# Windowed attention with a gated feed-forward layer: the probabilities of units 3 to 15 turned by VectorE and a DRAM round trip instead of TensorE

## Chip, cores and metric

One core of one Trainium2 chip runs the whole program. The metric is the device time of one execution in microseconds (us). The kernel before took 1105.88 us (median of three runs, 1104.23 to 1106.31).

## Reference

Inputs q, k, v are float32 of shape (8, 8, 576, 64): batch, head, position, head dimension. Heads 0 to 3 look back over a plain window of 32 positions, heads 4 to 7 over 32 positions four apart. The attention output, laid out as 4608 tokens of 512 features, goes through an RMS norm and a gated feed-forward layer of width 1536.

```python
scores = scale * np.matmul(q, k.transpose(0, 1, 3, 2))
mask_plain = (rel >= 0) & (rel < window)
mask_dil = (rel >= 0) & (rel < window * dilation) & (rel % dilation == 0)
scores = np.where(masks[None, :, :, :], scores, -1000000000.0)
attn = np.exp(scores - max); attn = attn / (sum + 1e-09)
x = np.matmul(attn, v)            # then tokens x 512
xn = x / rms * rms_g
out = (silu(xn @ w_gate) * (xn @ w_val)) @ w_out
```

## The kernel before, in words

The 4608 tokens are cut into 16 units of 288 (half a batch element each). Unit u's attention runs while unit u-1's feed-forward layer is on TensorE, so attention is the side work and the feed-forward matmuls fill TensorE.

**Feed-forward.** A unit takes 36 steps: for each of 12 column blocks j a gate step, a val step and a proj step (`gate`, `val`, `proj`). From unit 1 on, each step is 12 matmuls of 288 columns (L679, L682): numbers are split into a high and a low float32r part and three products are summed. VectorE works in it at L724 (silu), L737 (product), and in the norm; ScalarE at L719 (tanh) and L748 (high part); GpSimd at L749 (low part).

**Attention bursts.** A unit has 14 bursts; a burst (u, c, i) is a block of 96 or 72 queries of two heads. Bursts with c = 0, 1 are plain (96 queries, 128 or 96 keys), those with c = 2, 3 are dilated (72 queries; 104 keys in odd units, 72 in even ones). The small matmuls of a burst stand at the end of a step. With q the step of its scores:

- step q: scores (`scored`, L524), into the one PSUM buffer `s`;
- q+1: `scores_max` on VectorE: L381 adds the mask to the low product, L386 (once for each head, with a read of the accumulator behind it) adds the high product and keeps the row's extreme. The result is tile `t` (96 x 2 x 128);
- q+2: exponential on ScalarE (L401);
- q+4: sum and reciprocal on VectorE (L410, L411), scaling by it on GpSimd (L417);
- q+6: two TensorE transposes against an identity (`transposed`, L497) into a part of PSUM; from there ScalarE copies the high part (L477) and VectorE subtracts for the low part (L479) into `pt`, in which keys are the partitions;
- q+10: probabilities times values (`output`, L512); at q+11 VectorE adds up the four partial results into `xraw` (`take`, L439 and L441, once for each head).

From unit 3 on the scores of a unit's bursts are two steps apart, from 11 steps before the feed-forward of the unit ahead of it begins to step 15 of that (`EARLY`, `LAST`); `BEHIND` sets the two later places. The first three units take other schedules and plain float32 products.

**Order.** The order of every engine is written by hand: `later(dt, rank, fn)` puts work into the flush at the beginning of step now+dt, sorted by rank; the engines run their queues in order. All DMAs are issued from SP: a query/key tile for each head (L293), a value tile for each burst (`load_v`, L301), the outputs (L777). `split` makes high and low parts of queries and keys, `split_v` those of the values.

Of the kernel before, what the change touches and what calls it, by code (L numbers as in the profile page):

```python
# [57 lines left out]
EARLY, LAST = -11, 15  # L58
BEHIND = 6, 10
DONE = 25  # L60
# [17 lines left out]
def attn_moe(ctx: ExitStack, tc: tile.TileContext, qk_in, v_in, w_gate, w_val, w_out, rms_g, outT):  # L78
# [7 lines left out]
    sb = ctx.enter_context(tc.tile_pool(name="sb", bufs=2))  # L86
    ps = ctx.enter_context(tc.tile_pool(name="ps", bufs=1, space=PSUM))


# [224 lines left out]
    def split_v(b, dt):  # L314
        k = everything.index(b) % 2

        def hi():
            if k not in vparts:
                vparts[k] = late[0].tile([P, 2, 2, D], F32R, name=f"vhl_{k}", bufs=1)
            A.copy(out=vparts[k][:, :, 0], in_=vs[b])  # L320

        def lo():
            vp = vparts[k]
            G.tensor_tensor(out=vp[:, :, 1], in0=vs.pop(b), in1=vp[:, :, 0], op=ALU.subtract)  # L324
            load_v(further(b, 3))

        later(dt, 3.3, hi)
        later(dt, 5.1, lo)
# [6 lines left out]
    def split(u, h, when, ek, eq):  # L335


        raw = heads[u, h]
        _, _, nkt = geometry(u, h // 2)
        qr, kr = raw[:, :U], raw[:, U:U + nkt]  # L340
        got = []

        def tile(cols, tag):
            pool, bufs = (late[0], 1) if late and h % 4 == 3 else (sb, 3)
            return pool.tile([P, cols], F32R, tag=tag, name=f"{tag}_{u}_{h}", bufs=bufs)

        def k_hi():
            ks = tile(2 * KW, "ks").rearrange("p (t k) -> p t k", t=2)
            A.copy(out=ks[:, 0, :nkt], in_=kr)
            got.append(ks)  # L350

        def k_lo():
            ks = got[0]
            ek.tensor_tensor(out=ks[:, 1, :nkt], in0=kr, in1=ks[:, 0, :nkt], op=ALU.subtract)  # L354

        def q_hi():
            qs = tile(U, "qs")
            A.copy(out=qs, in_=qr)  # L358
            got.append(qs)

        def q_lo():
            ks, qs = got
            eq.tensor_tensor(out=qs[D:], in0=qr[D:], in1=qs[D:], op=ALU.subtract)  # L363
            heads[u, h] = (qs, ks)
            if after(u, h, 2):
                load(*after(u, h, 2))
# [7 lines left out]
    def scores_max(u, c, i, s_ps):  # L374
# [3 lines left out]
        other = u < NNAT and everything.index((u, c, i)) % 4 == 3  # L378
        t = sb.tile([QB, 2, P], F32, tag="qs" if other else "t", name=f"t_{u}_{c}_{i}", bufs=3)
        if u >= NEX:  # L380
            V.tensor_tensor(out=t[:nq, :, :n], in0=sv[:nq, :, 1, :n],  # L381
                            in1=mask[:nq, None, mc:mc + n].to_broadcast([nq, 2, n]), op=ALU.add)
        sm = sums[everything.index((u, c, i)) % len(sums)]
        for a in range(2):
            plus = t[:nq, a, :n] if u >= NEX else mask[:nq, mc:mc + n]
            V.tensor_tensor_reduce(out=t[:nq, a, :n], in0=sv[:nq, a, 0, :n], in1=plus,  # L386
                                   op0=ALU.add, op1=ALU.min,
                                   scale=-(0.5 if u == NNAT else 1.0) / math.sqrt(D),
                                   scalar=3e38, accum_out=sm[:nq, a, 0:1])
        st[u, c, i] = t, sm  # L390

    def by_rows(u, c, i):
# [3 lines left out]
    def scores_exp(u, c, i):  # L396
# [3 lines left out]
        for a in range(2):  # L400
            A.activation(out=t[:nq, a, :n], in_=t[:nq, a, :n], func=AF.Exp, scale=-1.0,  # L401
                         bias=sm[:nq, a, 0:1], accum_out=None if by_rows(u, c, i) else sm[:nq, a, 1:2])

    def scores_norm(u, c, i):
# [7 lines left out]
        for a in range(2):  # L412
            if u == 1:
                later(1, -0.5, lambda a=a: A.activation(out=t[:nq, a, :n], in_=t[:nq, a, :n], func=AF.Copy,
                                                        scale=sm[:nq, a, 3:4]))
                continue
            (V if u == 0 and (c, i) > (NC - 1, 1) else G).tensor_scalar(  # L417
                out=t[:nq, a, :n], in0=t[:nq, a, :n], scalar1=sm[:nq, a, 3:4],
                scalar2=1.0, op0=ALU.mult, op1=ALU.mult)
# [50 lines left out]

    def untranspose(b, t_ps, wait):
        blocks, nq, _ = geometry(*b[:2])
        n = blocks[b[2]][3]
        t_in = t_ps[:n].rearrange("k (a q) -> k a q", a=2)[:, :, :nq]
        exact = b[0] < NEX
        st[b] = pt = sb.tile([P, 2, 2, QB], F32 if exact else F32R, tag="pt", name=f"pt_{b[0]}_{b[1]}_{b[2]}", bufs=2)
        A.copy(out=pt[:n, 0, :, :nq], in_=t_in)  # L477
        def low_part():
            V.tensor_tensor(out=pt[:n, 1, :, :nq], in0=t_in, in1=pt[:n, 0, :, :nq], op=ALU.subtract)  # L479

        if not exact:
            later(1, 0.4 if wait > 1 else -1.5, low_part) if wait else low_part()

    def products(q, t, o, t_ps, s_tag="s", o_tag="o", wait=0):
# [41 lines left out]
        order = ((t, transposed), (o, output), (q, scored))  # L526
        if t and t[0] >= NEX:
            order = ((o, output), (t, transposed), (q, scored))
        parts = [(b, fn, a) for b, fn in order for a in range(2)]
# [3 lines left out]
        if t:  # L533
            later(1, 0.2, lambda: untranspose(t, t_ps, wait))
        if o:
# [5 lines left out]
            if o[0] < NEX:  # L541
                later(1, 9, lambda: load_v(further(o, 3)))
            far = further(o, 2)
            if far and far[0] >= NEX:
                split_v(far, 8 if o[0] < NEX else 1)
        if q:
# [3 lines left out]
            later(3 if q[0] < NNAT else 4, 1 if behind else -1, lambda: scores_norm(*q))  # L550
            u, c, i = q
            nxt = after(u, 2 * c, 2)
            nb = len(geometry(u, c)[0])
# [275 lines left out]
    for u in range(1, NU):  # L829
        q_at = [LAST - (LAST - EARLY) * (nb - 1 - k) // (nb - 1) for k in range(nb)]  # L830
        t_at, o_at = ([t + n for t in q_at] for n in BEHIND)
        if u <= NNAT:
# [25 lines left out]
    for u in range(NU):  # L858
        for j in range(NJ):
            for part in range(0 if u + j else 2, 3):  # L860
# [16 lines left out]
                else:  # L877
# [3 lines left out]
                    free = None  # L881
                if part == 2 or part == 1 and events.get(now[0], {}).get("t", (0,))[0] >= NEX:
                    if "t" in events.get(now[0], {}):
                        free = ps.tile([P, 512], F32, tag=bank("g", j), name=f"t_{u}_{j}")[:, :2 * QB]
                attend(free, s_tag="acc2" if t < 4 else "s", wait=(1, 2, 0)[part])
# [71 lines left out]
```

## Time and profile before

| | before |
|---|---|
| median of 3 runs | 1105.88 us |
| profiled execution | 1103.95 us |
| its span, first to last instruction | 1102.2 us |
| TensorE matmul busy | 1095.2 us (99%) |
| VectorE busy | 782.7 us (71%) |
| ScalarE busy | 614.8 us (56%) |
| GpSimd busy | 670.1 us (61%) |
| 16 DMA engines, share of the span | 24.3% |

PE is TensorE's matmul side, DVE is VectorE, ACT ScalarE, POOL GpSimd, SP the engine that issues DMAs. A share over the span is a mean over fuller and emptier stretches; the view of windows gives the busy time in any stretch, and the view of waits gives what an engine waited for there. From some 164 us to the end of the span a unit takes about 66 us, 18 burst places of two steps each, of which 14 carry bursts.

### The profile page before, as it was taken

The numbers are of one execution on the slowest core, as the hardware profiler recorded it, in microseconds if no ns is written. First come the engines' busy times: TensorE is split into PE (matmuls) and PEld (weight loads), VectorE is DVE, ScalarE is ACT, GpSimd is POOL, SyncE is SP. The second block draws the span as 40 slices with busy tenths as digits, with TensorE's granted clock in tenths as the row PEclk, the third lists the DMA queues.
The fourth block names the chain that finished last, engine by engine and source line by source line (L and its number), as shares of the span: only waits on it lengthen the run. The fifth ranks groups of instructions, "written<-read, shape, count | busy, mean of one in ns | idle before, by whom it ended". The sixth has DMA issues, their size and how long they took to land.

```text
span 1102.2 us, 25627 instructions
## 1 busy us (share of the span) xinstructions
PE 1095.2 (99%) x8416; PEld 1071.6 (97%) x8416; DVE 782.7 (71%) x3094; ACT 614.8 (56%) x2202; POOL 670.1 (61%) x1152
## 2 busy tenths in 40 slices
PE   8999999999999999999999999999999999999998
PEld 7787999999999999999999999999999999999998
DVE  7988667868687676867768677686867768687412
ACT  6895676556465564646556464664646556464211
POOL 6333589657585675757657575775758657584211
PEclk9999999999999999999999999999999999999999
DMA  9774213212131131312212131131212212120000
GB/s 255 205 263 163 79 51 87 74 35 82 43 94 52 41 97 30 95 42 73 66 36 85 43 94 43 50 96 37 79 43 83 64 32 83 53 74 13 18 6 22
DMA packets 61543, 82.18 MB, mean 75 GB/s; under 512 B 7298, under 2 KB 41090, under 8 KB 61410
## 3 DMA queue, kind: packets, MB, share of 16 engines
q1 hardware_dynamic: 61410, 80.54, 24.3%
q8 instruction: 67, 1.10, 0.4%
q14 instruction: 66, 0.54, 0.2%
HBM read 71.08 MB, written 9.44 MB: 73 GB/s over the span
## 4 chain that ended last, share of the span: by engine, by line
PE 95%; POOL 2%; DVE 1%; ACT 1%; issue 1%; POOLq 0%; ACTq 0%; DVEq 0%
PE acc L682 17%; PE g L682 17%; PE v L682 17%; PE acc L679 9%; PE g L679 9%; PE v L679 9%; PE o L512 3%; PE s L524 3%; PE acc L676 2%; PE v L676 2%; PE g L676 2%; PE t L497 2%; PE s L521 1%; PE g L497 1%; PE busy L802 1%; PE o L509 1%
## 5 line engine op out<-in xcount | busy, mean ns | idle before, releaser
L749 POOL TENSOR_TENSOR hlo<-th,hhi 128x288 fp32r<-128x288 f32 x179 | 145.2, 811 | 161.3 <-ACT hhi L748 147.8
L401 ACT ACTIVATE t<-t,sum 96x128 f32<-96x128 f32 (+3 forms) x448 | 165.9, 374 | 107.8 <-DVE sum L386 105.1
L682 PE MATMUL acc<-hhi,lo 128*128 128x288 f32 x720 | 212.7, 295 | 0.0
L417 POOL TENSOR_SCALAR t<-t,sum 96x128 f32<-96x128 f32 (+3 forms) x416 | 147.6, 366 | 88.4 <-DVE sum L411 74.6
L719 ACT ACTIVATE th<-g 128x288 f32<-128x288 f32 x180 | 73.8, 410 | 195.2 <-PE g L682 100.5
L682 PE MATMUL g<-xhi,lo 128*128 128x288 f32 x612 | 180.3, 295 | 0.0
L682 PE MATMUL v<-xhi,lo 128*128 128x288 f32 x612 | 180.2, 294 | 0.0
L439 DVE TENSOR_REDUCE xraw<-o 64x72 f32<-64x144 f32 (+1 forms) x364 | 117.1, 322 | 84.0 <-PE o L512 79.5
L724 DVE SCALAR_TENSOR_TENSOR th<-th,g 128x288 f32<-128x288 f32 x180 | 80.8, 449 | 102.0 <-ACT th L719 78.4
L682 PEld LDWEIGHTS acc<-hhi,lo 128*128 128x128 f32 x720 | 135.4, 188 | 0.0
L324 POOL TENSOR_TENSOR vhl<-vt,vhl 128x128 fp32r<-128x128 f32 x182 | 84.4, 464 | 70.4 <-ACT vhl L320 66.8
L748 ACT CAST hhi<-th 128x288 fp32r<-128x288 f32 x180 | 77.7, 432 | 75.5 <-DVE th L737 74.6
L682 PEld LDWEIGHTS g<-xhi,lo 128*128 128x128 f32 x612 | 115.2, 188 | 0.0
L682 PEld LDWEIGHTS v<-xhi,lo 128*128 128x128 f32 x612 | 115.1, 188 | 0.0
L737 DVE TENSOR_TENSOR th<-th,v 128x288 f32<-128x288 f32 x180 | 79.8, 444 | 43.6 <-PE v L682 43.5
L441 DVE TENSOR_TENSOR xraw<-o,xraw 64x72 f32<-64x72 f32 (+1 forms) x364 | 101.1, 278 | 12.5
L679 PE MATMUL acc<-hhi,hi_o 128*128 128x288 f32 x360 | 109.0, 303 | 0.0
L679 PE MATMUL g<-xhi,hi_g 128*128 128x288 f32 x357 | 107.0, 300 | 0.0
L682 PE MATMUL acc<-hlo,hi_o 128*128 128x288 f32 x360 | 106.4, 296 | 0.0
L363 POOL TENSOR_TENSOR qs<-qk,qs 64x288 fp32r<-64x288 f32 x104 | 84.3, 811 | 24.1 <-ACT qs L358 16.9
L354 POOL TENSOR_TENSOR ks<-qk,ks 128x288 fp32r<-128x288 f32 (+2 forms) x104 | 96.8, 936 | 3.1
L682 PE MATMUL g<-xlo,hi_g 128*128 128x288 f32 x322 | 95.1, 295 | 0.0
(193 smaller groups left out, 3458.6 us busy)
## 6 DMA issues: line engine op xcount, KB each, us to landing
qk<-in_qk_dram SPq DMA_DIRECT2D x60, 288.0 KB, 2.9
vt<-in_v_dram SPq DMA_DIRECT2D x196, 64.0 KB, 1.9
qk<-in_qk_dram SPq DMA_DIRECT2D x30, 352.0 KB, 2.9
out_dram<-ot SPq DMA_DIRECT2D x64, 144.0 KB, 1.9
qk<-in_qk_dram SPq DMA_DIRECT2D x30, 304.0 KB, 2.9
raw<-in_w_gate_dram SPq DMA_DIRECT2D x12, 512.0 KB, 4.6
raw<-in_w_val_dram SPq DMA_DIRECT2D x12, 512.0 KB, 3.3
raw<-in_w_out_dram SPq DMA_DIRECT2D x12, 512.0 KB, 4.2
```

Source lines behind the costliest of these rows:

```text
L324: G.tensor_tensor(out=vp[:, :, 1], in0=vs.pop(b), in1=vp[:, :, 0], op=ALU.subtract)
L354: ek.tensor_tensor(out=ks[:, 1, :nkt], in0=kr, in1=ks[:, 0, :nkt], op=ALU.subtract)
L363: eq.tensor_tensor(out=qs[D:], in0=qr[D:], in1=qs[D:], op=ALU.subtract)
L401: A.activation(out=t[:nq, a, :n], in_=t[:nq, a, :n], func=AF.Exp, scale=-1.0, bias=sm[:nq, a, 0:1], accum_out=None if by_rows(u, c, i) els ...
L417: (V if u == 0 and (c, i) > (NC - 1, 1) else G).tensor_scalar(out=t[:nq, a, :n], in0=t[:nq, a, :n], scalar1=sm[:nq, a, 3:4], scalar2=1.0, ...
L439: V.tensor_reduce(out=ours, in_=o[:D, cols:cols + 2 * nq].rearrange("d (t q) -> d q t", t=2), axis=mybir.AxisListType.X, op=ALU.add)
L441: V.tensor_tensor(out=ours, in0=o[D:, cols:cols + nq], in1=ours, op=ALU.add)
L679: PE.matmul(out, wh[:, cc, :], xh, start=start, stop=False)
L682: PE.matmul(out, w[:, cc, :], v, start=False, stop=stop and k == 1)
L724: V.scalar_tensor_tensor(out=t, in0=t, scalar=1.0, in1=g, op0=ALU.add, op1=ALU.mult)
L737: V.tensor_tensor(out=t, in0=t, in1=v_ps[:, :U], op=ALU.mult)
L749: (V if (u, j) == (NU - 1, NJ - 1) else G).tensor_tensor(out=lo, in0=t, in1=hi, op=ALU.subtract)
```

## The change

From unit 3 on (`u >= NEX`) TensorE no longer transposes the probabilities. Instead, in `turn`:

- `scores_max` writes the keys of a row interleaved by four: key 4i+c goes to column 32c+i. L381's and L386's successors write, and the second also reads, tile `t` in steps of 32 elements. Where a burst has fewer than 96 queries or 128 keys, VectorE first sets the whole tile to zero (96 x 256).
- q+5: VectorE transposes `t` in place in squares of 32 by 32 (96 x 256), rank 4, behind `scores_max` of the burst two places later (rank 0.7).
- q+5, rank 9.5: SP sends the tile to DRAM (192 rows of 512 bytes).
- q+6, rank 9.5: SP fetches it into `pt` (128 partitions, 6 pieces of 128 bytes each).
- q+9: ScalarE makes the high part (rank 0.2) and VectorE the low part (rank 0.9), both now out of SBUF. The output stays at q+10.

`t` gets a fourth buffer, the value tile has two buffers instead of three, and the loads of values and of queries and keys are issued a step later, at rank 9.9, behind the fetch.

```diff
-BEHIND = 6, 10
+OUTPUT = 10
+TURN = (5, 4), (5, 9.5), (6, 9.5), (9, 0.2), (9, 0.9)
...
-            vt = sb.tile([P, 2, D], F32, tag="vt", name=f"vt_{u}_{c}_{i}", bufs=3)
+            vt = sb.tile([P, 2, D], F32, tag="vt", name=f"vt_{u}_{c}_{i}", bufs=2)
...
-            load_v(further(b, 3))
+            later(1, 9.9, lambda: load_v(further(b, 2)))
...
         if u >= NEX:
-            V.tensor_tensor(out=t[:nq, :, :n], in0=sv[:nq, :, 1, :n],
-                            in1=mask[:nq, None, mc:mc + n].to_broadcast([nq, 2, n]), op=ALU.add)
+            if nq < QB or n < P:
+                V.memset(t, 0.0)
+            tk = keys(t, n)
+            V.tensor_tensor(out=tk[:nq], in0=sv[:nq, :, 1, :n].rearrange("q a (i c) -> q a i c", c=4),
+                            in1=mask[:nq, mc:mc + n].rearrange("q (i c) -> q i c", c=4)[:, None].to_broadcast(
+                                [nq, 2, n // 4, 4]), op=ALU.add)
...
+    def keys(t, n):
+
+        return t.rearrange("q a (c i) -> q a i c", i=W)[:, :, :n // 4]
...
+    def turn(b):
+        blocks, nq, _ = geometry(*b[:2])
+        n = blocks[b[2]][3]
+        got = []
+
+        def squares():
+            t = st[b][0]
+            V.transpose(out=t, in_=t)
+
+        def put():
+            t, _ = st.pop(b)
+            d = dr.tile([2, QB, P], F32, tag="turn", name=f"turn_{b[0]}_{b[1]}_{b[2]}")
+            nc.sync.dma_start(out=d.rearrange("a q k -> q a k"), in_=t)
+            got.append(d)
+
+        def get():
+            st[b] = pt = sb.tile([P, 2, 2, QB], F32R, tag="pt", name=f"pt_{b[0]}_{b[1]}_{b[2]}", bufs=2)
+            squares = got.pop().rearrange("a (r i) (c j) -> (i c) (a r) j", i=W, j=W)
+            nc.sync.dma_start(out=pt[:, 1].bitcast(F32).rearrange("k a (r j) -> k (a r) j", j=W), in_=squares)
...
+        for (dt, rank), fn in zip(TURN, (squares, put, get, high, low)):
+            later(dt, rank, fn)
```

VectorE, in unit 7's attention, from the last plain bursts to the third dilated one (t is a burst's scores and later its probabilities, with c and i in the name; o the output in PSUM; pt the turned probabilities), before:

```order
L439 TENSOR_REDUCE xraw_0_6861<-o_0_2_6992 64x96
L441 TENSOR_TENSOR xraw_0_6861<-o_0_2_6992,xraw_0_6861 64x96
L724 SCALAR_TENSOR_TENSOR th_1_6999<-th_1_6999,g_1_6978 128x288
L381 TENSOR_TENSOR t_2_1_7008<-s_2_1_6991,mask 72x2x104
L386 ISA t_2_1_7008,sum_86<-s_2_1_6991,t_2_1_7008 72x104
L386 ISA sum_86 72x1
L386 ISA t_2_1_7008,sum_86<-s_2_1_6991,t_2_1_7008 72x104
L386 ISA sum_86 72x1
L479 TENSOR_TENSOR pt_1_1_7001<-g_1_6978,pt_1_1_7001 128x192
L410 TENSOR_REDUCE sum_90<-sum_90 72x2
L411 RECIPROCAL sum_90<-sum_90 72x2
L737 TENSOR_TENSOR th_1_6999<-th_1_6999,v_1_7022 128x288
```

The same place now, beginning at the silu:

```order
L767 SCALAR_TENSOR_TENSOR th_1_7118<-th_1_7118,g_1_7099 128x288
L387 MEMSET t_2_1_7126 96x256
L389 TENSOR_TENSOR t_2_1_7126<-s_2_1_7112,mask 72x2x26x4
L398 ISA t_2_1_7126,sum_88<-s_2_1_7112,t_2_1_7126 72x26x4
L398 ISA sum_88 72x1
L398 ISA t_2_1_7126,sum_88<-s_2_1_7112,t_2_1_7126 72x26x4
L398 ISA sum_88 72x1
L521 TENSOR_TENSOR pt_1_0_7014<-pt_1_0_7014 128x192
L502 STREAM_TRANSPOSE t_1_2_6980<-t_1_2_6980 96x256
L427 TENSOR_REDUCE sum_92<-sum_92 72x2
L428 RECIPROCAL sum_92<-sum_92 72x2
L780 TENSOR_TENSOR th_1_7118<-th_1_7118,v_1_7141 128x288
```

The zeroing (L387) and the squares (L502) have come in, and the low part (L521, before L479) now belongs to the burst whose output is the next on TensorE, one burst later than before.

TensorE, at the end of a proj step of the same unit (s_2_2 are the scores of the burst after), before:

```order
L682 MATMUL acc_3_7064<-hhi_0_6924,lo_1009 128x288
L512 MATMUL o_1_0_7070<-pt_1_0_6922,vhl_2337 128x192 x2
L497 MATMUL t_1_7068<-ident,t_1_2_6869 128x96 x2
L524 MATMUL s_2_2_7069<-ks_4_6741,qs_4_6768 72x2x104
L524 MATMUL s_2_2_7069<-ks_5_6766,qs_5_6805 72x2x104
L679 MATMUL g_2_7093<-xhi_0_6732,hi_o_1008 128x288
```

and now:

```order
L725 MATMUL acc_3_7186<-hhi_0_7039,lo_1011 128x288
L555 MATMUL o_1_0_7191<-pt_1_0_7014,vhl_2335 128x192 x2
L567 MATMUL s_2_2_7190<-ks_4_6853,qs_4_6882 72x2x104
L567 MATMUL s_2_2_7190<-ks_5_6880,qs_5_6917 72x2x104
L722 MATMUL g_2_7215<-xhi_0_6844,hi_o_1010 128x288
```

Only the two transposes have gone; the output and the scores stand where they stood.

SP, loads around the same bursts (turn is the tile in DRAM, vt the values, qk a head's queries and keys), before:

```order
L293 DMA qk_6_6803<-in_qk_dram 128x704
L293 DMA qk_7_6838<-in_qk_dram 128x704
L301 DMA vt_1_2_6875<-in_v_dram 128x128
L301 DMA vt_2_0_6940<-in_v_dram 128x128
L777 DMA out_dram<-ot_0_6959 128x288
```

and now:

```order
L295 DMA qk_6_6954<-in_qk_dram 128x704
L507 DMA turn_1_0_6988<-t_1_0_6849 96x2x128
L295 DMA qk_7_6990<-in_qk_dram 128x704
L513 DMA pt_1_0_7014<-turn_1_0_6988 128x6x32
L303 DMA vt_1_1_7016<-in_v_dram 128x128
L507 DMA turn_1_1_7058<-t_1_1_6911 96x2x128
L820 DMA out_dram<-ot_0_7076 128x288
```

For each burst a DMA to DRAM and one back have come in, the way back behind a wait for the way there, and the loads of later tiles stand between them.

More of the change, by code (lines that the diff above doesn't have):

```diff
@@ L365, in q_lo @@
             if after(u, h, 2):
-                load(*after(u, h, 2))
+                later(1, 9.9, lambda: load(*after(u, h, 2)))
         for dt, rank, fn in zip(when, (3, 5, 3.1, 0.9 if when[3] > when[2] else 3.2), (k_hi, k_lo, q_hi, q_lo)):
@@ L378, in scores_max @@
         other = u < NNAT and everything.index((u, c, i)) % 4 == 3
-        t = sb.tile([QB, 2, P], F32, tag="qs" if other else "t", name=f"t_{u}_{c}_{i}", bufs=3)
+        if late and everything.index((u, c, i)) % 4 == 3:
+            t = late[0].tile([QB, 2, P], F32, tag="t", name=f"t_{u}_{c}_{i}", bufs=1)
+        else:
+            t = sb.tile([QB, 2, P], F32, tag="qs" if other else "t", name=f"t_{u}_{c}_{i}", bufs=3)
         if u >= NEX:
-            V.tensor_tensor(out=t[:nq, :, :n], in0=sv[:nq, :, 1, :n],
-                            in1=mask[:nq, None, mc:mc + n].to_broadcast([nq, 2, n]), op=ALU.add)
+            if nq < QB or n < P:
[4 more added lines that the diff above has]
+                                [nq, 2, n // 4, 4]), op=ALU.add)
         sm = sums[everything.index((u, c, i)) % len(sums)]
         for a in range(2):
-            plus = t[:nq, a, :n] if u >= NEX else mask[:nq, mc:mc + n]
-            V.tensor_tensor_reduce(out=t[:nq, a, :n], in0=sv[:nq, a, 0, :n], in1=plus,
+            out, scores, plus = t[:nq, a, :n], sv[:nq, a, 0, :n], mask[:nq, mc:mc + n]
+            if u >= NEX:
+                out = plus = tk[:nq, a]
+                scores = scores.rearrange("q (i c) -> q i c", c=4)
+            V.tensor_tensor_reduce(out=out, in0=scores, in1=plus,
                                    op0=ALU.add, op1=ALU.min,
@@ L400, in scores_exp @@
         for a in range(2):
-            A.activation(out=t[:nq, a, :n], in_=t[:nq, a, :n], func=AF.Exp, scale=-1.0,
+            e = t[:nq, a, :n] if u < NEX else t[:nq, a].rearrange("q (c i) -> q c i", i=W)[:, :, :n // 4]
+            A.activation(out=e, in_=e, func=AF.Exp, scale=-1.0,
                          bias=sm[:nq, a, 0:1], accum_out=None if by_rows(u, c, i) else sm[:nq, a, 1:2])
@@ L416, in scores_norm @@
                 continue
+            e = t[:nq, a, :n] if u < NEX else t[:nq, a].rearrange("q (c i) -> q c i", i=W)[:, :, :n // 4]
             (V if u == 0 and (c, i) > (NC - 1, 1) else G).tensor_scalar(
-                out=t[:nq, a, :n], in0=t[:nq, a, :n], scalar1=sm[:nq, a, 3:4],
+                out=e, in0=e, scalar1=sm[:nq, a, 3:4],
                 scalar2=1.0, op0=ALU.mult, op1=ALU.mult)
@@ L469, in attn_moe, with untranspose, high, low @@
     everything = [b for u in range(NU) for b in bursts(u)]
-    def untranspose(b, t_ps, wait):
+    def untranspose(b, t_ps):
         blocks, nq, _ = geometry(*b[:2])
         n = blocks[b[2]][3]
[L474 to L482, printed above, removed]
+        st[b] = pt = sb.tile([P, 2, 2, QB], F32, tag="pt", name=f"pt_{b[0]}_{b[1]}_{b[2]}", bufs=2)
+        A.copy(out=pt[:n, 0, :, :nq], in_=t_ps[:n].rearrange("k (a q) -> k a q", a=2)[:, :, :nq])
+    def turn(b):
[14 more added lines that the diff above has]
+            nc.sync.dma_start(out=pt[:, 1].bitcast(F32).rearrange("k a (r j) -> k (a r) j", j=W), in_=squares)
+        def high():
+            pt = st[b]
+            A.copy(out=pt[:n, 0, :, :nq], in_=pt[:n, 1, :, :nq].bitcast(F32))
+        def low():
+            pt = st[b]
+            V.tensor_tensor(out=pt[:n, 1, :, :nq], in0=pt[:n, 1, :, :nq].bitcast(F32), in1=pt[:n, 0, :, :nq],
+                            op=ALU.subtract)
+        for (dt, rank), fn in zip(TURN, (squares, put, get, high, low)):
+            later(dt, rank, fn)
     def products(q, t, o, t_ps, s_tag="s", o_tag="o", wait=0):
@@ L533, in products @@
         if t:
-            later(1, 0.2, lambda: untranspose(t, t_ps, wait))
+            later(1, 0.2, lambda: untranspose(t, t_ps))
         if o:
@@ L881, in attn_moe @@
                     free = None
-                if part == 2 or part == 1 and events.get(now[0], {}).get("t", (0,))[0] >= NEX:
-                    if "t" in events.get(now[0], {}):
-                        free = ps.tile([P, 512], F32, tag=bank("g", j), name=f"t_{u}_{j}")[:, :2 * QB]
+                if part == 2 and "t" in events.get(now[0], {}):
+                    free = ps.tile([P, 512], F32, tag=bank("g", j), name=f"t_{u}_{j}")[:, :2 * QB]
                 attend(free, s_tag="acc2" if t < 4 else "s", wait=(1, 2, 0)[part])
```

12 lines of the change are left out of this document (7 added, 5 removed).

## The prediction

> **What bounds the kernel now.** I read the page first: the busy times and the chain that ended last.
>
> ```profile
> PE 1095.2 (99%) x8416; PEld 1071.6 (97%) x8416; DVE 782.7 (71%) x3094; ACT 614.8 (56%) x2202; POOL 670.1 (61%) x1152
> PE 95%; POOL 2%; DVE 1%; ACT 1%; issue 1%; POOLq 0%; ACTq 0%; DVEq 0%
> ```
>
> TensorE bounds it: 95% of the chain, hardly ever idle. So an instruction taken from TensorE is worth its whole place there, as long as nothing else becomes late. The second question is therefore who has room for the work that takes its place. The view of windows, for unit 7's bursts in three stretches and for the middle stretch of unit 8:
>
> ```profile
> core 0: us, PE busy (x) PEld busy (x) DVE busy (x) ACT busy (x) POOL busy (x), PEclk, DMA share, GB/s
> 427.91:446.35 18.44, 18.44 (x146) 18.44 (x145) 12.06 (x48) 12.14 (x41) 12.03 (x20) 1.00 0.17 48
> 446.35:479.98 33.63, 33.63 (x272) 33.63 (x271) 28.15 (x123) 20.59 (x79) 26.19 (x46) 1.00 0.31 91
> 479.98:493.99 14.01, 14.01 (x113) 14.01 (x111) 9.08 (x35) 4.92 (x17) 6.30 (x12) 1.00 0.08 20
> 512.34:545.67 33.33, 33.33 (x273) 33.33 (x271) 27.19 (x123) 20.00 (x79) 25.06 (x46) 1.00 0.30 90
> ```
>
> VectorE's 71% is uneven. In the middle stretch, nine burst places long, it is busy for 28.15 of 33.63 us; outside it has 6.4 and 4.9 us over. And not all of the missing 5.5 us is free. The view of waits for VectorE, first in the odd unit's middle stretch, then in the even one's:
>
> ```profile
> DVE xraw L439 <- PE o L512: 2.6, 5, 0.9
> DVE th L737 <- PE v L682: 0.8, 3, 0.3
> DVE xlo L660 <- ACT xhi L659: 0.2, 1, 0.2
> ```
>
> ```profile
> DVE xraw L439 <- PE o L512: 3.1, 5, 1.0
> DVE th L737 <- PE v L682: 1.1, 3, 0.5
> DVE xlo L660 <- ACT xhi L659: 0.2, 1, 0.2
> ```
>
> It waits for only 3.6 us in the odd unit and 4.4 us in the even one; the rest are the small steps between instructions that follow each other. That wait is what VectorE can still take on before TensorE waits for it: 0.4 to 0.5 us a burst.
>
> **What is removed.** The transposes of units 3 to 15:
>
> ```profile
> 160.00:1102.00 942.00, 56.00 (x364) 36.23 (x364) 1.00 0.20 58
> 459.27 0.37 PE L512 MATMUL o<-pt,vhl 128*128 128x192 f32 x2
> 459.48 0.33 PE L497 MATMUL t<-ident,t 96*128 96x96 f32 x2
> 459.59 0.41 PE L524 MATMUL s<-ks,qs 128*72 128x208 f32 x2
> 602.38 0.29 PE L497 MATMUL t<-ident,t 72*104 72x72 f32 x2
> 602.48 0.39 PE L524 MATMUL s<-ks,qs 128*72 128x208 f32 x2
> ```
>
> The first row is the window of line 497 alone: 364 of them, two for each of 182 bursts. Their 56 us busy overlap with their neighbours, so what a pair holds up TensorE is read from start to start: 0.11 us for a plain pair, 0.10 us for a dilated one. 6 of 14 bursts are plain: 78 x 0.11 + 104 x 0.10 = 19 us. That is all the change can win. The copies and the low parts stay (SBUF in place of PSUM as their source, which I cost at nothing; ScalarE, at 20.59 of 33.63 us, covers its own). GpSimd's scaling stays too.
>
> **What is added on VectorE.** Its prices come from the groups by form:
>
> ```profile
> L381 DVE TENSOR_TENSOR t<-s,mask 96x256 f32<-96x256 f32 x66 | 27.5, 417 | 1.2
> L381 DVE TENSOR_TENSOR t<-s,mask 72x208 f32<-72x208 f32 x56 | 20.6, 368 | 1.1
> L386 DVE CUSTOM_DVE_ANT_0 t<-s,t 96x128 f32<-96x128 f32 x132 | 32.9, 284 | 2.3
> L386 DVE CUSTOM_DVE_ANT_0 t<-s,t 72x72 f32<-72x72 f32 x96 | 18.3, 226 | 1.6
> L263 DVE MEMSET qk<- 64x576 f32 x3 | 1.6, 538 | 1.1 <-PEq L945 0.9
> L441 DVE TENSOR_TENSOR xraw<-o,xraw 64x72 f32<-64x72 f32 x208 | 60.5, 291 | 7.2
> L441 DVE TENSOR_TENSOR xraw<-o,xraw 64x96 f32<-64x96 f32 x156 | 40.6, 260 | 5.4
> L435 ACT COPY xraw<-o 64x72 f32<-64x72 f32 x32 | 9.2, 287 | 1.8 <-PE o L509 1.5
> L435 ACT COPY xraw<-o 64x96 f32<-64x96 f32 x24 | 5.6, 232 | 0.2
> ```
>
> *Squares.* No transpose by VectorE is in this trace. The nearest row has the same 96 x 256 elements: 0.42 us. Bounds: 0.33 us, if an operation with one source has a shorter start, and 0.8 us if these elements take two passes. I take 0.42, nine times in the middle stretch: 3.8 us.
>
> *Zeroing.* 96 x 256, in every dilated burst. The only row is 64 x 576 in 0.538 us; by the number of elements 0.24 us; bounds 0.12 us (twice the rate) and 0.33 us. Eight in the stretch: 1.9 us.
>
> *Writing in steps of 32 elements.* No row has that step. Two rows of this kernel have a step of 4 elements, in the 72-query bursts: `take`'s L441 needs 0.291 us for 72 elements in steps against 0.260 us for 96 side by side. L386 loses 58 ns for 56 fewer elements, 1.04 ns each; so 72 side by side would have cost L441 0.235 us, and the step costs 56 ns, 0.78 ns an element. ScalarE's L435 shows the same sign, 0.287 against 0.232 us. If 0.78 ns holds for the add (208 elements in odd units) and for the two halves behind it (2 x 104), a dilated burst pays 0.32 us; in even units (144 and 2 x 72) 0.225 us; a plain one 0.4 us. In the middle stretch (one plain, eight dilated): 3.0 us odd, 2.2 us even. Bounds: nothing, and twice this. I take the row's price.
>
> [...]
>
> *Sum on VectorE in a middle stretch.* Odd units: 3.8 + 1.9 + 3.0 = 8.7 us. Free: 3.6 us less the 9 x 0.1 us by which TensorE gets shorter, 2.7 us. Missing: 6.0 us. Even: 7.9 against 3.5 us, missing 4.4 us. Outside the middle stretch the 6.4 and 4.9 us hold what comes in (five bursts' squares and steps, some 4 us, and two squares).
>
> When VectorE is late, who waits? Its queue runs in order, and an output on TensorE now waits for the low part, which stands behind zeroing, the add and the two halves of a later burst in one flush. So TensorE waits at the output, with scores and feed-forward behind it. A little lateness is covered:
>
> ```profile
> 458.39 0.08 DVE L386 DVE_READ_ACCUMULATOR2_ANT sum<- 72x1 f32 x1
> ```
>
> The scores were taken up by 458.47 us and the next ones wrote their buffer at 459.59, 1.1 us later; with the burst's own zeroing and steps (0.5 us) in between I leave 0.5 us of it once in a unit. So 5.5 us in each of 7 odd units and 3.9 us in each of 6 even ones: 62 us.
>
> **What is added on the queues.**
>
> ```profile
> qk<-in_qk_dram SPq DMA_DIRECT2D x60, 288.0 KB, 2.9
> vt<-in_v_dram SPq DMA_DIRECT2D x196, 64.0 KB, 1.9
> out_dram<-ot SPq DMA_DIRECT2D x64, 144.0 KB, 1.9
> DMA  0000000000000000000000335667541000000000
> DMA packets 144, 0.07 MB, mean 33 GB/s; under 512 B 16, under 2 KB 144, under 8 KB 144
> ```
>
> The way there is like an output: 1.9 us. The way back is 768 pieces of 128 bytes. The last two rows are a window of 2 us around one value tile (128 pieces of 512 bytes): about ten slices of 0.05 us, 0.5 us. Between 1.9 us (a value tile's landing, if the number of pieces costs nothing) and 4.4 us (640 more pieces at that pace, 2.5 us) I take 3 us. With 0.3 us for the high part the chain from the squares to the low part is 4.1 to 6.6 us. VectorE gets to that low part two burst places later (2 x 33.63 / 9 = 7.5 us) less one low part and one squares (some 0.8 us): 6.7 us. So I cost the round trip at nothing; if it lasts longer, ScalarE waits in its queue at the high part, with the exponentials and high parts of the feed-forward behind it. On SP the fetch waits for the landing of the way there, and the loads of values and queries stand behind it. A value tile is wanted some two steps (3.7 us) after its load can go, against 1.9 us. The zeroing waits until the way there has read the buffer's last tile; with four buffers that is some two steps earlier.
>
> **The sum.** 1103.95 (the profiled execution) - 19 + 62 = 1147 us. The median before stands 2 us above that execution, less than the doubt in any price.
>
> **Rivals.**
>
> *VectorE has room; TensorE stays the bound.* Squares at 0.33, zeroing at 0.12 us and a step that is free make 9 x 0.33 + 8 x 0.12 = 3.9 us: 0.7 us missing in odd units after the 0.5 us, none in even ones, 5 us in all: 1103.95 - 19 + 5 = 1090 us. It turns at a gain when the missing time falls under 19 us, that is about 0.56 us added a burst. For it: 71% busy, and all three prices from other operations. Against it: L441, and that the squares alone, at 0.42 us, take more than is free in an odd unit's middle stretch.
>
> *The round trip is late.* If the fetch goes at a value tile's pace and, in the 8 of 14 bursts with a query load on the queue beside it, lands another 1.0 us later (2.9 against 1.9 us), then the low part is late by 1.0 us in 104 bursts: 1103.95 - 19 + 104 = 1189 us. It decides from a landing of about 4.4 us after the issue on. For it: the pieces are 128 bytes, where no row here goes under 512 apart from the DMAs' last words; against it: the DMA engines are used to 0.31 at most. [...]
>
> *Both sides meet.* Missing time of 19 us would leave the time as it is.
>
> **Chances.** VectorE the bound: 0.57, of it 0.42 with the step priced as above (1147 us; at twice that price 7 x 3.0 + 6 x 2.2 = 34 us more, 1181; with squares in two passes 13 x 9 x 0.38 = 44 us more, 1191) and 0.15 with a free step (34 us less, 1113). Room on VectorE, 1090: 0.20. Round trip late, 1189 or more: 0.18. Level: 0.05. Range 1090 to 1215 us: it leaves out the faster half of the second case and the far end of the third. Faster by over 0.2% (2 us, what a measurement here can tell): 0.20; within: 0.05; slower: 0.75.
>
> **What would show it.** In the profile after: no transposes of units 3 to 15 on PE; PE with idle time at the outputs, released by VectorE's low part; in the middle stretches VectorE full, with waits near zero, and the stretch longer by 3 to 5 us than before. The squares near 0.42 us, the add of a dilated odd burst near 0.37 + 0.16 = 0.53 us, the zeroing near 0.24 us. ScalarE's high part should seldom wait for the DMA. I am wrong if PE stays full (then the prices were too high), or if the waits at the output come from the high part and the DMA.

## The result, and the profile after

| | before | after |
|---|---|---|
| median (4 runs each) | 1105.09 us | 1188.24 us (1187.89 to 1191.32) |
| ratio to before, 95% interval | | 1.0758, 1.0736 to 1.0780 |
| profiled execution, span | 1103.95, 1102.2 us | 1187.89, 1185.7 us |
| forecast | | 1147 us, 1090 to 1215 |

The kernel became 83 us slower. The forecast had the direction and the engine; it had 41 us too little. The page of the kernel after, busy times and chain:

```profile
PE 1109.9 (94%) x8052; PEld 1051.8 (89%) x8052; DVE 942.8 (80%) x3392; ACT 627.5 (53%) x2202; POOL 674.1 (57%) x1152
PE 46%; DVE 41%; issue 7%; ACT 3%; DMA 2%; POOL 1%; DVEq 0%; POOLq 0%; ACTq 0%; SPq 0%
```

TensorE has lost its 364 transposes, and with them its place as the only bound: of the chain that ended last, VectorE now has 41%, where it had 1%. The view of windows, for the same three stretches of unit 7 and the middle stretch of unit 8 as in the prediction:

```profile
452.52:470.91 18.39, 18.32 (x143) 18.08 (x141) 14.06 (x49) 11.63 (x41) 12.03 (x20) 1.00 0.24 63
470.91:510.86 39.95, 34.76 (x254) 32.66 (x253) 36.60 (x139) 21.26 (x80) 26.66 (x47) 1.00 0.47 115
510.86:525.71 14.85, 14.11 (x107) 13.75 (x105) 10.88 (x40) 5.55 (x18) 6.50 (x13) 1.00 0.37 84
544.24:582.58 38.34, 34.49 (x255) 32.43 (x254) 34.99 (x139) 21.15 (x80) 25.04 (x47) 1.00 0.48 116
```

The middle stretches are 6.3 and 5.0 us longer, and VectorE is busy in them for 8.45 us more (28.15 to 36.60) and 7.80 us more (27.19 to 34.99). In both, the view of VectorE's waits is empty: it goes from one piece to the next. Who waits instead, in the view of waits over the whole span:

```profile
ACT pt L517 <- DMA pt<-turn: 56.8, 77, 2.7
PE o L555 <- DVE pt L521: 51.3, 83, 1.1
PEld o L555 <- issue: 43.8, 62, 1.3
PEld o L555 <- POOL vhl L326: 15.7, 17, 1.3
PEld g L722 <- DVE th L780: 19.6, 52, 0.5
```

L555 is the output, L521 the low part. In the records of the single instructions, each of 106 late outputs began at most 0.3 us after the end of a low part, most of them 0.26 us after it, 74 us of TensorE in all. So the rows listed under "issue" and under the value parts are for the most part the same wait (the value parts had been ready 3.6 us and more). Another 16 us of idle time stand at the gate steps, which wait for VectorE's product (L780). The prices, in the groups by form of the kernel after:

```profile
L502 DVE STREAM_TRANSPOSE t<-t 96x256 f32<-96x256 f32 x182 | 78.9, 433 | 0.0
L387 DVE MEMSET t<- 96x256 f32 x116 | 31.6, 272 | 7.9
L389 DVE TENSOR_TENSOR t<-s,mask 72x208 f32<-72x208 f32 x56 | 30.4, 543 | 6.2 <-DVE t L387 0.5
L398 DVE CUSTOM_DVE_ANT_1 t<-s,t 72x72 f32<-72x72 f32 x96 | 23.3, 282 | 1.6
```

Squares 0.433 us (forecast 0.42), zeroing 0.272 (0.24), the add of a dilated odd burst 0.543 (0.53). There are 116 zeroings: one for each of the 104 dilated bursts, and 12 for plain bursts with 96 keys, which the prediction left out. Seven of them, not eight, fall into unit 7's middle stretch; the eighth begins at 511.01 us, just behind its end. The round trip, in the view of DMA issues, with the median from issue to landing in the last column:

```profile
turn<-t SPq DMA_DIRECT2D x182, 96.0 KB, 1.8
pt<-turn SPq DMA_DIRECT2D x182, 96.0 KB, 2.2
vt<-in_v_dram SPq DMA_DIRECT2D x196, 64.0 KB, 2.1
```

The way back (96 KB) lands in 2.2 us, about as fast as a value tile (64 KB, 2.1 us).

One price stands in no row above. The low part used to read one of its two sources from PSUM; now it reads both from SBUF. The low part of the norm (`xlo`, L660 before, L703 after) reads both from SBUF in either kernel. Such a piece took longer in these traces when it began while GpSimd was in a subtraction of its own with over 0.16 us to go. The same two pieces of unit 7, GpSimd's (`ks`) and VectorE's (`xlo`), in the view of the timeline, first before:

```profile
447.89 0.46 DVE L660 TENSOR_TENSOR xlo<-xraw,xhi 128x288 fp32r<-128x288 f32 x1 [0.18 <-ACT xhi L659]
447.92 1.37 POOL L354 TENSOR_TENSOR ks<-qk,ks 128x416 fp32r<-128x416 f32 x1
```

and after:

```profile
472.94 1.08 POOL L356 TENSOR_TENSOR ks<-qk,ks 128x416 fp32r<-128x416 f32 x1
473.06 1.28 DVE L703 TENSOR_TENSOR xlo<-xraw,xhi 128x288 fp32r<-128x288 f32 x1
```

Whichever of the two began second was the longer for it: GpSimd's took 1.37 us in place of 1.08, VectorE's 1.28 in place of 0.46. All 7 odd units have the longer `ks` before (1.37 to 1.38 us) and the longer `xlo` after (1.28 to 1.29). Of the 182 low parts of the bursts none took over 0.36 us before, though 144 had a piece of GpSimd beside them and 117 began inside one; now 78 begin inside one, and 30 of these take between 0.40 and 0.91 us, each ended at least 0.16 us after that piece. Of the other 48 one began together with GpSimd's piece, the rest in its last 0.16 us, and none took over 0.37 us. The 182 together take 67.5 us in place of 58.0. No run moved GpSimd's pieces alone, so what this is worth in the end is not measured.

### The profile page after: what moved, and what is told of

Read it like the earlier page. It is cut to its first block, busy times and chain, and to the rows that moved or that the text cites. A ratio compares the mean times of both kernels' runs of the same rounds, so it can differ in the third digit from the quotient of the medians.

```text
span 1185.7 us, 26525 instructions
## 1 busy us (share of the span) xinstructions
PE 1109.9 (94%) x8052; PEld 1051.8 (89%) x8052; DVE 942.8 (80%) x3392; ACT 627.5 (53%) x2202; POOL 674.1 (57%) x1152
## 4 chain that ended last, share of the span: by engine, by line
PE 46%; DVE 41%; issue 7%; ACT 3%; DMA 2%; POOL 1%; DVEq 0%; POOLq 0%; ACTq 0%; SPq 0%
PE g L725 8%; PE v L725 8%; PE acc L725 7%; DVE xraw L457 6%; DVE t L389 6%; DVE xraw L459 5%; PE g L722 4%; PE v L722 4%; PE acc L722 3%; DVE t L398 3%; DVE pt L521 3%; DVE th L780 3%; DVE t L502 3%; DVE th L767 3%; DVE t L387 3%
## 5 line engine op out<-in xcount | busy, mean ns | idle before, releaser
L435 POOL TENSOR_SCALAR t<-t,sum 96x128 f32<-96x128 f32 (+3 forms) x416 | 150.3, 373 | 200.8 <-DVE sum L428 170.9
L457 DVE TENSOR_REDUCE xraw<-o 64x72 f32<-64x144 f32 (+1 forms) x364 | 116.5, 320 | 35.1 <-PE o L555 29.4
L767 DVE SCALAR_TENSOR_TENSOR th<-th,g 128x288 f32<-128x288 f32 x180 | 80.8, 449 | 79.7 <-ACT th L762 64.7
L555 PE MATMUL o<-pt,vhl 128*128 128x192 f32 (+3 forms) x364 | 73.1, 283 | 58.8 <-DVE pt L521 51.3
L555 PEld LDWEIGHTS o<-pt,vhl 128*128 128x128 f32 (+3 forms) x364 | 55.7, 188 | 80.5 <-issue 43.8
L326 POOL TENSOR_TENSOR vhl<-vt,vhl 128x128 fp32r<-128x128 f32 x182 | 88.3, 485 | 65.3 <-ACT vhl L322 55.3
L398 DVE CUSTOM_DVE_ANT_1 t<-s,t 96x128 f32<-96x128 f32 (+3 forms) x364 | 109.8, 341 | 6.2
L722 PE MATMUL g<-xhi,hi_g 128*128 128x288 f32 x357 | 109.4, 306 | 4.1 <-DVE th L780 2.5
L389 DVE TENSOR_TENSOR t<-s,mask 96x256 f32<-96x256 f32 (+3 forms) x182 | 98.5, 541 | 13.3 <-DVE t L387 0.9
```

Of the source, the lines that this page charges most:

```text
L389: V.tensor_tensor(out=tk[:nq], in0=sv[:nq, :, 1, :n].rearrange("q a (i c) -> q a i c", c=4), in1=mask[:nq, mc:mc + n].rearrange("q (i c) - ...
L398: V.tensor_tensor_reduce(out=out, in0=scores, in1=plus, op0=ALU.add, op1=ALU.min, scale=-(0.5 if u == NNAT else 1.0) / math.sqrt(D), scala ...
L457: V.tensor_reduce(out=ours, in_=o[:D, cols:cols + 2 * nq].rearrange("d (t q) -> d q t", t=2), axis=mybir.AxisListType.X, op=ALU.add)
L555: PE.matmul(o_ps[:, 2 * a * nq:2 * (a + 1) * nq].rearrange("d (t q) -> d t q", t=2), vp[:n, a].rearrange("k t d -> k (t d)"), pt[:n, :, a, ...
L722: PE.matmul(out, wh[:, cc, :], xh, start=start, stop=False)
L767: V.scalar_tensor_tensor(out=t, in0=t, scalar=1.0, in1=g, op0=ALU.add, op1=ALU.mult)
```

## The experiments

Two theories were set against each other: *VectorE's row* (what was added to VectorE no longer fits between the outputs) and *the round trip* (the fetch lands late and the high part with it). Times are medians; before on the same chips was between 1104.1 and 1104.5 us.

**All of VectorE's additions away, round trip kept.** The scores side by side, no zeroing (four `t` buffers stay and are filled with zeros once), no squares, so the probabilities are not turned:

```diff
-                V.memset(t, 0.0)
-            V.tensor_tensor(out=tk[:nq], ...)        # steps of 32
+            V.tensor_tensor(out=t[:nq, :, :n], ...)  # side by side
-            V.transpose(out=t, in_=t)
```

> The changed kernel without what came in on VectorE: no squares, no zeroing (the buffers are zeroed once at the start), keys written side by side; the round trip through DRAM and all queues as in the changed kernel. It leaves out the turning, so the probabilities are not transposed. If VectorE's time is the whole cause: the 19 us of the transposes are won, some 1085 to 1092 us, and TensorE is busy again almost throughout. If the round trip or the later loads are the cause: it stays above 1150 us.

1088.84 us, ratio 0.9857 (0.9822 to 0.9892). The middle stretches of units 7 and 8:

```profile
440.09:473.34 33.25, 32.90 (x255) 32.48 (x254) 29.28 (x122) 20.95 (x79) 26.44 (x46) 1.00 0.55 138
505.07:537.73 32.66, 32.62 (x255) 32.13 (x254) 28.50 (x120) 20.36 (x79) 25.07 (x46) 1.00 0.57 138
```

The round trip, the fourth buffer and the later loads are all in this kernel, and it is 15.3 us faster than before (two executions): that is what leaving out TensorE's transposes gave, less whatever the round trip costs here (forecast 19 us). The other 99.4 us (1188.24 - 1088.84) came in with VectorE's additions.

**A fetch that needn't wait for its own way there.** It reads the DRAM tile that the burst before has written, out of four:

```diff
-    dr = ctx.enter_context(tc.tile_pool(name="dr", bufs=2, space=bass.MemoryType.DRAM))
+    dr = ctx.enter_context(tc.tile_pool(name="dr", bufs=4, space=bass.MemoryType.DRAM))
...
-            got.append(d)
+            got.append(sent[-1] if sent else d)
+            sent.append(d)
```

> The changed kernel, but the fetch takes the DRAM tile of the burst before (four DRAM tiles), so it does not wait for its own burst's way there; all bytes still move. It computes with the probabilities of another burst. VectorE as the cause: 1188 us within 5. Round trip as the cause of the part that the forecast missed: some 40 us less, 1147 us.

1188.32 us, ratio 1.0757 (1.0726 to 1.0789): nothing. ScalarE's waits for the fetch, 56.8 us in the kernel after, are gone in this one, and the time has not moved. For the changed kernel the theory of the round trip falls.

**Steps away alone:**

```diff
-            tk = keys(t, n)
-            V.tensor_tensor(out=tk[:nq], ...)
+            V.tensor_tensor(out=t[:nq, :, :n], ...)
```

> The changed kernel with keys written side by side instead of in steps of 32; everything else stays, so the keys come out in another order than the values. VectorE as the cause: by the changed kernel's rows the steps cost 3.1 us in an odd unit's middle stretch and 2.3 us in an even one's, 7 x 3.1 + 6 x 2.3 = 35 us, so some 1152 us, and the add of 96 x 256 back at 0.42 us. Otherwise: within 5 us of 1188.

1148.44 us, ratio 1.0396 (1.0366 to 1.0426): 39.8 us less, a little more than the 35 expected.

**Squares away alone:**

```diff
-            V.transpose(out=t, in_=t)
+            pass
```

> The changed kernel without the squares alone (the probabilities are not transposed). VectorE as the cause: 9 x 0.43 us in each of 13 middle stretches, 50 us, so some 1138 us. Round trip as the cause: its chain begins 0.43 us earlier, so at most 0.43 x 104 bursts, 45 us, but with ScalarE's waits for the fetch shorter and VectorE's queue without waits no longer; then e2 must fall as well.

1163.21 us, ratio 1.053 (1.0499 to 1.0561): 25 us less, half of what was expected. Two rows of its waits over the whole span say where the rest went:

```profile
DVE xraw L457 <- PE o L555: 46.8, 52, 1.6
PEld o L555 <- issue: 38.7, 72, 1.0
```

VectorE waits for outputs again (46.8 us; with the squares 29.4), and outputs still wait. A full row is not the whole of it: output, sums, zeroing, add, halves, low part, next output form a ring in which the two engines wait for each other, and the squares stand beside a part of that ring. That reading is argued from the order of the pieces; no run took the ring apart.

**The loads as early as before**, not a step later (two value buffers stay):

```diff
-            later(1, 9.9, lambda: load_v(further(b, 2)))
+            load_v(further(b, 2))
-                later(1, 9.9, lambda: load(*after(u, h, 2)))
+                load(*after(u, h, 2))
```

> The loads of a burst's values and of a head's queries and keys are issued as soon as their buffer is free, as before the change, not one step later; the squares, the zeroing, the steps of 32 and the round trip stay. Theory VectorE's work on the path: the loads are not waited for on the path (the waits on a value tile, 26 us in 39 places, are ScalarE's, which has time): 0 to 4 us less, 1184 to 1190. Theory later loads: the value parts come late to TensorE, which the waits on GpSimd's value part at the output show (listed as POOL vhl): 20 to 30 us less, 1158 to 1168.

1201.19 us, ratio 1.0882 (1.0865 to 1.0898): 13 us *more*; neither theory had it. The waits in SP's queue, first of the kernel after, then of this one (L295 is the load of queries and keys, L507 the way to DRAM, L513 the fetch):

```profile
SPq L513 <- DMA turn<-t: 277.9, 166, 3.5
SPq L507 <- DVE sum L428: 240.0, 138, 4.4
SPq L295 <- POOL qs L365: 54.4, 38, 5.2
```

```profile
SPq L513 <- DMA turn<-t: 298.0, 145, 4.3
SPq L295 <- POOL qs L365: 219.4, 90, 5.4
SPq L507 <- DVE sum L428: 21.4, 33, 1.7
```

A load that is issued before its buffer is free holds up SP here (L295 waits 219.4 us in place of 54.4), and the way to DRAM behind it: L507 hardly waits for the squares any more (21.4 us in place of 240.0; the view puts that wait down to L428, two pieces behind them in VectorE's queue), because it gets its turn after them. ScalarE's waits for the fetch grow from 56.8 to 157.9 us. So in the changed kernel the later loads keep these 13 us away.

**The zeroing on GpSimd.**

```diff
-                V.memset(t, 0.0)
+                G.memset(t, 0.0)
```

> The zeroing of t goes from VectorE to GpSimd, all else as in the changed kernel. Theory VectorE's work on the path: 116 pieces of 272 ns, some 0.3 us with their issue, leave its row; nearly all of them lie in the middle stretches, eight per unit, directly between the two sums of one output and the add of the next, so all of their time is on the path: 30 to 35 us less, 1153 to 1160 us, and the middle stretch of unit 7 falls from 39.95 to about 37.5 us. Theory latency (what is on the path is the number of steps from output to output, not VectorE's sum): the zeroing has no part in what the output waits for once it is elsewhere, but the add would now wait for GpSimd, which is behind its own row: less than 15 us, 1175 to 1190.

1213.9 us, ratio 1.0993 (1.0978 to 1.1008): 26 us more. The row of its waits:

```profile
DVE t L389 <- POOL t L387: 76.9, 77, 2.2
```

The 31.6 us of zeroing left VectorE's row, and 76.9 us of waiting for GpSimd came in: the zeroing stands behind GpSimd's scalings and low parts, and VectorE stops at the add until it is done.

**The zeroing away alone.** Four `t` buffers stay:

```diff
+    tiles, count = [cst.tile([QB, 2, P], F32, name=f"t_{k}") for k in range(3)], [0]   # ... and a fourth later
+    for t in tiles:
+        G.memset(t, 0.0)
...
-                V.memset(t, 0.0)
```

> The changed kernel without the zeroing: four t buffers stay and are filled with zeros once at the start, squares, steps of 32 and round trip are as in the changed kernel. Nothing waits for a zeroing on another engine now. Theory VectorE's row: 8 pieces of 0.272 us and their gaps, some 2.4 us, leave a middle stretch and 1 piece a tail: 30 to 34 us less, 1154 to 1159 us; unit 7's middle stretch 37.5. Theory latency from output to output: the zeroing, like the squares, counts half, 1170 to 1175 us.

1147.38 us, ratio 1.0386 (1.0373 to 1.0399): 40.9 us less, more than either theory said and more than the 31.6 us that the zeroing is busy. Shared out over the 116 zeroings that is 0.35 us each.

**The zeroing at another place of VectorE's own row**, a step earlier:

```diff
+            if q[0] >= NEX:
+                zeroed[q] = fresh(*q)          # allocates t, V.memset(t, 0.0)
             later(1, 0.7, lambda: scores_max(*q, s_ps))
```

> The changed kernel with the same zeroing on VectorE, issued a step earlier: it stands ahead of the output's sums in VectorE's row, behind the squares of the step before, no longer between the sums and the add. VectorE does the same work. Theory sum of VectorE's row: 1183 to 1193 us, no gain. Theory latency from output to output (what counts in full is what stands between the sums of one output and the low part of the next; what stands elsewhere, like the squares, costs some half or a third): the zeroing costs 10 to 15 us in place of 41, so 1158 to 1170.

1156.45 us, ratio 1.0472 (1.0454 to 1.0489): 31.8 us less with the same instructions on VectorE, a little more than the second theory said. The chain of waits shows what the place does. In the kernel after, silu (L767), product (L780), the four sums of an output, the zeroing (L387), the add (L389); the columns are start, duration and what:

```profile
478.05 0.36 DVE th L767
478.41 0.03 issue
478.44 0.02 DVEq L780
478.46 0.04 issue
478.50 0.46 DVE th L780
...
479.91 0.26 DVE xraw L459
480.17 0.11 issue
480.28 0.28 DVE t L387
480.57 0.03 issue
480.59 0.02 DVEq L389
480.61 0.04 issue
480.66 0.55 DVE t L389
```

And in this kernel (L776 silu, L386 zeroing, L789 product, L466 the last sum, L396 the add):

```profile
467.69 0.34 DVE th L776
468.04 0.00 issue
468.04 0.06 DVE t L386
468.10 0.14 issue
468.23 0.39 DVE th L789
...
469.57 0.26 DVE xraw L466
469.83 0.03 issue
469.87 0.57 DVE t L396
```

From the last sum's end to the add's start the kernel after needs 0.49 us (480.17 to 480.66), this one 0.04 (469.83 to 469.87). Between silu and product it needs 0.19 us in place of 0.09, so in this burst the zeroing costs 0.10 us in place of some 0.45: part of it lies where VectorE stood still anyway. 116 times the difference are 41 us; 31.8 of them come out at the end.

**Squares alone.** Keys in natural order and no zeroing; row p of the fetched tile is then key 32(p mod 4) + p/4, and the values are laid out that way (the high part, the low part and the output then go over all 128 partitions):

```diff
+                    at = _np.arange(P) if u < NEX else _np.arange(P) % 4 * W + _np.arange(P) // 4
+                    v_in[u, c, at < n, i, a] = v[b, h, ki[kc:kc + n]][at[at < n]]
```

> Probabilities lie in natural key order (no steps of 32), nothing is zeroed, four t buffers stay and are filled with zeros once; the squares and the round trip stay. Row p of the fetched tile is then key 32 (p mod 4) + p / 4, and the values of the later units are laid out in that order in their input. Theory VectorE's sum on the path: 1089 us (the run without squares, steps and zeroing) plus 13 times 9 squares of 0.47 us = 1089 + 55 = 1144 if each is on the path, less the 7 us per unit that TensorE still had to spare there (stretch 33.25 against VectorE's work), so 1115 to 1144. Theory half of the squares lies beside the latency from output to sum: about 0.25 us each, as when they alone were left out: 1110 to 1118. Additive prices (1188 less 40 for the steps, less 30 for the zeroing): 1118.

1117.47 us, ratio 1.0116 (1.0102 to 1.0130). It lies in the ranges of both theories and so decides nothing between them. The squares alone cost 28.6 us over the bare kernel's 1088.84, and that is more than the transposes gave. Not all of it need be VectorE's own time. The squares also stand ahead of the way to DRAM, and two rows of this kernel's waits are larger than in the kernel after (56.8 and 0.6 us there):

```profile
ACT pt L521 <- DMA pt<-turn: 135.9, 125, 3.3
DVE pt L525 <- ACT pt L521: 19.7, 28, 1.4
```

The low part now waits for the high part, and the high part for the fetch; of the chain that ended last, DMA has 6% here and 2% in the kernel after. A fetch that needn't wait was not tried in this kernel, so how much of the 28.6 us is the round trip's is open.

**The low part of every burst on GpSimd besides**, in the kernel with the squares alone:

```diff
-            V.tensor_tensor(out=pt[:, 1, :, :nq], ..., op=ALU.subtract)
+            G.tensor_tensor(out=pt[:, 1, :, :nq], ..., op=ALU.subtract)
```

> [...] Theory VectorE's sum on the path: VectorE then has per burst the square (0.43) more and the low part (0.38) less than with neither, so the middle stretches fall back to about 33 us: 1087 to 1098, faster than before by 6 to 17 us. Theory latency: GpSimd takes longer for the low part (its 96x128 pieces take over 0.5 us) and has the value parts, splits and scalings in the same row, so the output waits for GpSimd instead: 1105 to 1130.

1112.4 us, ratio 1.0072 (1.0059 to 1.0085). GpSimd's scalings of 96 x 128 took 0.39 us in the mean in the kernel after (units 3 to 15; 0.58 at most), not over 0.5 as the second theory had it. VectorE has room again, as its wait shows, and the outputs wait for GpSimd:

```profile
DVE xraw L461 <- PE o L559: 78.5, 95, 3.0
PEld o L559 <- POOL pt L525: 30.8, 45, 1.7
PE o L559 <- POOL pt L525: 19.0, 31, 1.4
```

**The low part of every second burst on GpSimd:**

```diff
+            (V if everything.index(b) % 2 else G).tensor_tensor(out=pt[:, 1, :, :nq], ...)
```

> As the kernel with squares alone, with the low part of every second burst on GpSimd. VectorE (1117 with all on it) and GpSimd (1112 with all on it) are each relieved of half. Theory VectorE's row: its additions are then 9 x 0.43 less 4.5 x 0.4, some 2 us in a middle stretch, which the 3.6 us that it waited there before hold: 1090 to 1100. Theory latency through GpSimd: every second output still waits for GpSimd's row, 1103 to 1110.

1109.68 us, ratio 1.0043 (1.0029 to 1.0057): the nearest to before, and still slower. Of the chain that ended last VectorE has 14%, DMA 7% and GpSimd 5%, so the round trip's part is open here too.

**All low parts on GpSimd, one of two scalings on ScalarE:**

```diff
+            if u >= NEX and a:
+                A.activation(out=e, in_=e, func=AF.Copy, scale=sm[:nq, a, 3:4])
+                continue
```

> As the kernel with squares alone and the low part on GpSimd, with one of the two scalings of a burst's probabilities by ScalarE in GpSimd's place. Theory GpSimd's row (busy 30.5 of 35.0 us in unit 7's middle stretch with the low parts, chain 19%): nine scalings of 0.5 us leave it, about 26 us stay, and the outputs find their low parts: 1088 to 1100. Theory order, not sum: the low part stands behind other work that waits for ScalarE, and ScalarE's row becomes longer by 9 x 0.37 us: 1108 to 1120.

1160.19 us, ratio 1.0502 (1.0489 to 1.0516), far above both. One row of its waits:

```profile
ACT t L440 <- DVE sum L432: 257.3, 180, 2.9
```

ScalarE has 47% of the span free in the kernel after, but it comes to the scaling long before VectorE's reciprocal is there, and everything behind it in its queue waits. It was room by the sum, and none by the order.

**The runs as one account.** Without additions 1088.84; with the squares 1117.47 (+28.6, the longer waits for the fetch with them); with the steps too 1147.38 (+29.9); with the zeroing too 1188.24 (+40.9): 99.4 us. Added in another order, the steps cost 39.8 (after the zeroing) and the zeroing 31.0 (before the steps): what comes last finds no room left.

For unit 7's middle stretch the same can be read off VectorE's records: from the end of one piece to the end of the next, added up by line (waits of a piece count with it; the same pieces in every column, apart from what came in; us):

| | before | bare | squares | squares, steps | after | zeroing ahead |
|---|---|---|---|---|---|---|
| sums of outputs | 14.07 | 13.08 | 11.82 | 11.30 | 11.26 | 10.57 |
| zeroing | - | - | - | - | 2.47 | 2.19 |
| add | 3.02 | 3.02 | 3.02 | 4.45 | 5.21 | 4.44 |
| halves | 4.51 | 4.52 | 4.52 | 5.97 | 5.88 | 5.95 |
| squares | - | - | 3.19 | 3.19 | 3.19 | 3.18 |
| low part | 2.58 | 4.03 | 3.29 | 3.79 | 2.51 | 3.15 |
| rest | 9.04 | 8.54 | 9.04 | 8.81 | 8.82 | 8.09 |
| sum | 33.22 | 33.19 | 34.88 | 37.51 | 39.34 | 37.57 |

The squares are 0.354 us in the row (they overlap with their neighbours' ends by 0.08), the steps 2.88 us (1.43 in the add, 1.45 in the halves), the zeroing 3.23 us: 2.47 itself and 0.76 in the add, which begins 0.10 us after the zeroing's end (the median of the 116). The column after has seven zeroings, the last column eight. The low part goes up and down with GpSimd's pieces beside it, and "rest" holds the norm's low part: 0.64 us before, 0.37 bare, 1.2 in the other four.

## Why the prediction was right, and where it was too low

- *TensorE saves 19 us.* 15.3 us (the bare kernel, with the round trip in it). Near.
- *VectorE is the engine without room, and TensorE waits at the output for the low part, which stands behind zeroing, add and halves.* Shown: the waits at L555, VectorE's empty waits in the middle stretches, and the bare kernel.
- *Squares 3.8 us in a middle stretch, steps 3.0, zeroing 1.9, 8.7 in all.* The busy time grew by 8.45 us. In the row: 3.2, 2.9 and 3.2, 9.3 in all. The zeroing is the mis-sized term: 3.2 us for seven, where 1.9 us was forecast for eight. Its price was taken from a lone zeroing, by elements; between the sums and the add it also has a gap ahead of it and holds up the add. Moving it took 31.8 us away.
- *Free: 2.7 us, and 0.5 us once in a unit.* The middle stretch should have grown by 5.5 - 0.9 = 4.6 us in odd units and 3.9 - 0.9 = 3.0 in even ones; it grew by 6.3 and 5.0. Of the odd unit's missing 1.7 us 0.6 is the price above (9.3 against 8.7), and another 0.6 is the norm's low part beside GpSimd (0.64 to 1.21 us in the row). What is left is the size of the 0.5 us, which were not there by this sum; no run measured them. In the even unit the bursts' low parts grew by 0.7 us (2.53 to 3.19).
- *The low parts stay, SBUF in place of PSUM as their source, at nothing.* This term was put at nothing without a row for it. With both sources in SBUF, 30 of the 182 low parts were prolonged beside GpSimd, where none had been before, and the 182 took 9.5 us more in all. How much of that reached TensorE was not measured; in the bare kernel the low parts took still longer, 82.7 us, where VectorE had room for it.
- *Outside the middle stretch the 6.4 and 4.9 us hold what comes in.* This step failed. With 0.1 us less for five bursts these stretches should have become 0.5 us shorter; they became 0.8 us longer in both units, mostly in the last one (14.01 to 14.85), where outputs still come. By that, a stretch with idle time on VectorE had room only where an output wasn't waiting. The account, with units 7 and 8 standing for all: 7 x 1.7 + 6 x 2.0 + 13 x 1.3 = 41 us, which is what the forecast lacked.
- *The round trip at nothing.* Right for the changed kernel: a fetch without its wait changed nothing there, and the landings were 1.8 and 2.2 us where 3 us had been taken for the way back. Its rival, 1189 us, would have given almost the measured time by another mechanism: only the runs tell the two apart. With less on VectorE the round trip does come into the chain, as the squares alone show.
- *The step, 0.78 ns an element.* Right. The add of 208 elements takes 543 ns in steps and took 368 without, 0.84 ns an element; a half of 72 elements 282 and 226 ns, 0.78. The free step, 1113 us among the chances, no run shows: without the steps the changed kernel was 39.8 us faster. No run had the step without the change of pattern that came with it (runs of four), so the two are priced together.
- *ScalarE's high part should seldom wait for the DMA.* Not so: it waited in 77 of 182 bursts, 56.8 us in all. But next to nobody waited for it in turn: VectorE's low part did so once, for 0.6 us, and with the fetch that needn't wait the 56.8 us are gone and the time is the same.

What stays open: why leaving the squares out gave 25 us and putting them in alone 28.6, when their row time is 0.35 us in each of 117 middle bursts (41 us), may lie in the waits that come back, in the round trip and in the pieces beside GpSimd; none of the three was measured by itself.

## What to carry to other kernels

Moving work from the engine that bounds to one at 71% is priced in the stretch where both are wanted, and there by the time from the end of one piece to the end of the next, with the gaps that a piece makes for its neighbours: the same zeroing cost 0.45 us between an output's sums and the add that overwrites its tile, and 0.10 us in front of a piece that waited anyway. Before such a piece goes to an emptier engine, look at what stands ahead of it in that engine's queue; of four such moves, each to an engine with about 40% of its time free, two cost 26 and 48 us, and two gained 5 and 8. A piece that now reads both its sources from SBUF must also be priced beside GpSimd's pieces: here 30 of 182 took 0.40 to 0.91 us, where none had taken over 0.36. And a load issued ahead of its free buffer was not early here: it held up its whole queue and cost 13 us.

## What was not expected of the hardware

- A VectorE subtraction with both sources in SBUF and a GpSimd subtraction get in each other's way in these traces, and the one that began second pays: VectorE's 1.28 us in place of 0.46, or GpSimd's 1.37 in place of 1.08. With one source in PSUM, none of VectorE's 182 low parts took over 0.36 us in the kernel before, though 117 of them began inside a piece of GpSimd.
- Pieces of 128 bytes: 768 of them (96 KB) landed in 2.2 us, a value tile of 64 KB in 2.1 us. The landing shows nothing of the size of the pieces, but the packets' records of the kernel after do: a piece of 128 bytes took a DMA engine 13 ns in the median, one of 512 bytes 27 ns, so a byte cost twice as much in the small ones.
- VectorE's pieces stood close behind each other or apart. In the kernel after, a zeroing behind silu began at silu's end (39 of them, within 4 ns); one behind an output's sums began 0.11 us after their end (the median of 71). In the kernel with the zeroing ahead it began at silu's end too (468.04), and the add, then next behind the sums, 0.04 us after their end. No run shows what decides it.
- Transposing 96 x 256 float32 values in squares of 32 took VectorE 433 ns by the record and 354 ns in the row (182 of them in the kernel after).
